# First product of the last layer pair as a block product for two of three token groups, and whole periods of the cosine written as integers by ScalarE

## Chip, cores and metric

One core of one Trainium2 chip runs the whole program in one launch. The metric is the device time of that launch in microseconds, lower is better; the number shown for a kernel is the median of several runs.

## What is computed

Three layers follow each other on 1152 tokens (2 x 576) of 512 channels: an attention with a bias from a small network, a mixture of four experts, and a last layer pair. The change touches the last pair alone:

```python
def _moe2_ref(x, w_in, w_out):      # x (1152, 512), w_in (512, 2048), w_out (2048, 512)
    h = x @ w_in
    g = h * np.cos(h)
    return (g @ w_out).astype(np.float32)
```

## The kernel before, in words

The program is written as a list of steps. A step names an engine, a duration that the author expects, what it reads and writes, and a function that issues its instructions. Graph.order() (line 107) is a planner: it plays the steps through with those expected durations, takes on each engine the ready step that stands first in the list, hands out buffers, and so fixes the order of instructions on every engine. Some steps may go to one of two engines; the planner decides. The engines run their queues in that order, and semaphores hold an instruction until its inputs are there. An instruction that waits holds all behind it on its engine.

Numbers of 32 bits are multiplied as pairs: a value is split into a high part (a copy rounded to the matmul's format) and a low part (the rest), and a product takes three matmuls: high x high, high x low, low x high. split (line 544) does that for weights: the high part on GpSimd or ScalarE (lines 546, 548), the low part on GpSimd or VectorE (line 549).

The experts' first product is done for most jobs as a block product (block_tokens line 804, block_weights line 856, block_job line 884): the tokens are cut into two column groups, the channels into two halves, the hidden units into two halves, and seven products of half size stand for eight, by Winograd's form of Strassen's rule. It needs sums of weights (S1 to S4), sums and differences of token groups (T1 to T4), and additions of products on VectorE (plus, line 906), some of which are kept in SBUF by ScalarE (keep_, line 902). Each block product is 6 matmuls (line 897).

The last pair goes in four pieces of 512 hidden units (jobs, line 1112, run by run_ff, line 764). In a piece, the three token groups of 384 (ALLG, line 985) take the first product plainly: l1_mm (line 750) is one step of 12 matmuls of 384 columns into one PSUM bank for 128 hidden units, four such steps a group. The second product l2_mm (line 756) is 12 matmuls of 512 columns for 128 tokens, three such steps a group, and follows one group behind. The first piece takes the token groups in reverse. Tokens come from the experts' layer in nine tiles of 128; each is transposed (line 972) and split into xh by ScalarE (line 975) and xl by VectorE (line 977).

Between the products stands m2_ev1 (line 1080), which makes h*cos(h). It finds the nearest whole number of periods by adding and subtracting a large constant (lines 1084 and 1086, ScalarE), takes 2 pi times that number away in two parts (lines 1088 and 1090, VectorE), takes the absolute value (1092) and the sine of pi/2 minus it (1093, both ScalarE), multiplies by h (1095, VectorE, reads PSUM) and splits the result (1096 ScalarE, 1097 VectorE). m2_ev2 (line 1102) adds up second products on VectorE (line 1108) and writes the output by DMA (line 1110).

Of the kernel before, what the change touches and what calls it, by code (L numbers as in the profile page):

```python
# [22 lines left out]
MAGIC = 12582912.0  # L23
# [312 lines left out]
def build(ctx: ExitStack, tc: tile.TileContext, consts, q, v, qd, kp, vp, w12, probs, mw1, mw2, win, wout, out):  # L336
# [28 lines left out]
    kc = T(sm, [128, 3], F32, "kc")  # L365
# [63 lines left out]
    G.step("DVE", 60, lambda: (nc.vector.memset(kc[:, 0:1], MAGIC), nc.vector.memset(kc[:, 1:2], float(np.pi / 2))), wr=[fix("kc")])  # L429
# [374 lines left out]
    def block_tokens(cols, keys, n, after):  # L804
# [4 lines left out]
        def block(d):  # L809
            ra, rb, rc, rd_ = [[(fix(nm), k) for nm in ("xh", "xl") for k in keys(dd, c)] for dd, c in ((d, 0), (d, 1), (d + 2, 0), (d + 2, 1))]  # L810
# [5 lines left out]
            def keep_(name, src, buf):  # L816
# [39 lines left out]
    def block_weights(srcs, after):  # L856

        fs = [Buf("F") for _ in range(4)]
        for f, src in zip(fs, srcs):
            dma(128 * 512 * 4, lambda f=f, src=src: nc.sync.dma_start(out=f.tile, in_=src), wr=[f], after=after)  # L860
        out = {}
        for d in range(2):
# [11 lines left out]
            for b, names in ((s12, ("S1", "S2")), (s34, ("S3", "S4")), (g, ("A12", "A22"))):  # L874
                h, l = Buf("W"), Buf("W")
                split(b, h, l, lambda h=h: h.tile, lambda l=l: l.tile, lambda b=b: b.tile, 512)
                for i, nm in enumerate(names):
                    out[nm, d] = (h, l), (lambda h=h, i=i: h.tile[:, 256 * i:256 * i + 256], lambda l=l, i=i: l.tile[:, 256 * i:256 * i + 256])
            h = Buf("W")
            split(f, h, h, lambda h=h: h.tile[:, lo_], lambda h=h: h.tile[:, hi_], lambda f=f: f.tile[:, lo_], 256)  # L880
            out["A11", d] = (h,), (lambda h=h: h.tile[:, lo_], lambda h=h: h.tile[:, hi_])
        return out

    def block_job(e, f0, cols, T_, n, gate):

        A = block_weights([mw1[e, 128 * i:128 * i + 128, f0:f0 + 512] for i in range(4)], [ends["bl"]] if "bl" in ends else gate)
        w2s = [load_w(mw2[e, f0 + 128 * i:f0 + 128 * i + 128, :], 512, (), [ends["l2"]]) for i in range(4)]
# [45 lines left out]
        ends["l1"] = ends["b1"]  # L933
        rd = [x for w in w2s for x in w[:2]]
# [97 lines left out]
    for i in blocked:  # L1032
        block_job(i // 2, 512 * (i % 2), bcols, tk, Q1, [last_l1[0]])
# [46 lines left out]
    def m2_ev1(n, z, hb):  # L1080
        h_, l_ = (lambda: hb.tile[:, 0:n]), (lambda: hb.tile[:, n:2 * n])
        m, r = Buf("F"), Buf("F")
        zz, mm_, rr = (lambda: z.tile[:, 0:n]), (lambda: m.tile[:, :n]), (lambda: r.tile[:, :n])
        G.step("ACT", t_act(n, 1), lambda: nc.scalar.activation(
            out=mm_(), in_=zz(), func=AF.Identity, scale=float(1 / (2 * np.pi)), bias=kc[:, 0:1]), rd=[z], wr=[m], new=[m, r])
# [4 lines left out]
        G.step("DVE", t_dve(n), lambda: nc.vector.scalar_tensor_tensor(  # L1090
            out=rr(), in0=mm_(), scalar=-C2, in1=rr(), op0=ALU.mult, op1=ALU.add), rd=[m, r], wr=[r], port=True)
# [10 lines left out]
    def m2_ev2(c, tt, y, c0, m):  # L1102
# [105 lines left out]
```

## Time and profile before

| | us |
|---|---|
| median of 3 runs | 810.33 (810.1 to 814.82) |
| span of the profiled execution, first to last instruction | 806.9 |
| TensorE busy | 787.3 |
| VectorE busy | 624.9 |
| ScalarE busy | 458.5 |
| GpSimd busy | 281.0 |
| last layer pair, from the first matmul of it to the last | 604.7 to 803.8 |

The profiled execution shows its span; what lies around it in a run is read as the difference to the median, 3.4 us. Busy times are from the profile: the time in which an engine had an instruction at work. Matmuls overlap in their pipeline, so a matmul's own duration says less than the distance between two.

### The profile page before, as it was taken

How to read it: one execution, taken by the hardware profiler on the slowest of the kernel's cores; microseconds unless marked ns; L12 is line 12 of the kernel's file. 1: busy time of each engine (PE TensorE's matmuls, PEld its weight loads, DVE VectorE, ACT ScalarE, POOL GpSimd, SP SyncE). 2: the span in 40 equal slices, each digit the busy share in tenths (PEclk: the TensorE clock that was granted, in tenths of full speed). 3: DMA queues.
4: the chain of work that ended last, by engine and by line, in shares of the span. 5: the costliest groups of instructions: out<-in, count | busy, mean ns of one | idle time of the engine just before them, and what ended most of it. 6: DMA issues, size and time to landing. Idle time of an engine off the chain costs nothing.

```text
span 806.9 us, 14934 instructions
## 1 busy us (share of the span) xinstructions
PE 787.3 (98%) x5190; PEld 654.6 (81%) x5190; DVE 624.9 (77%) x1376; ACT 458.5 (57%) x961; POOL 281.0 (35%) x292
## 2 busy tenths in 40 slices
PE   7899999999999999999999999999999999999998
PEld 5575667877888878888788888888889899998997
DVE  8969998888897887788887878777648655676664
ACT  6667547777786752335452626161428776675662
POOL 0110055658776873134451415050222130502200
PEclk9999999999999999999999999999999999999999
DMA  6978989877664520556434353444301110301112
GB/s 218 290 255 246 284 296 297 275 242 232 199 192 141 173 86 4 181 186 221 168 115 157 124 156 125 153 128 145 103 14 53 41 52 1 105 1 54 51 40 79
DMA packets 79275, 118.72 MB, mean 147 GB/s; under 512 B 12000, under 2 KB 37216, under 8 KB 79200
## 3 DMA queue, kind: packets, MB, share of 16 engines
q1 hardware_dynamic: 79200, 117.77, 45.5%
q8 instruction: 41, 0.67, 0.3%
q14 instruction: 34, 0.28, 0.1%
HBM read 96.00 MB, written 21.73 MB: 146 GB/s over the span
## 4 chain that ended last, share of the span: by engine, by line
PE 89%; DVE 7%; issue 2%; DMA 1%; ACT 1%; POOL 1%; SPq 0%; DVEq 0%; ACTq 0%; POOLq 0%
PE p1x L762 24%; PE p1x L753 11%; PE p L762 9%; PE p L753 9%; PE p1x L897 9%; PE p L700 4%; PE p L637 4%; PE p L506 4%; PE p L682 3%; PE p L897 3%; PE p L998 3%; PE p L1006 3%; PE p L658 1%; DVE es L514 1%; DVE es L521 1%
## 5 line engine op out<-in xcount | busy, mean ns | idle before, releaser
L762 PE MATMUL p1x<-wx,hs 128*128 128x512 f32 x882 | 205.9, 389 | 0.0
L762 PEld LDWEIGHTS p1x<-wx,hs 128*128 128x128 f32 x882 | 164.3, 188 | 33.4
L549 POOL TENSOR_TENSOR wx<-fs,wx 128x512 fp32r<-128x512 f32 (+1 forms) x82 | 100.3, 1234 | 28.3 <-ACT wx L548 26.0
L753 PE MATMUL p1x<-xh,wx 128*128 128x384 f32 (+2 forms) x344 | 97.3, 351 | 1.6 <-DVE hs L949 1.6
L546 POOL TENSOR_SCALAR wx<-fs 128x512 fp32r<-128x512 f32 (+1 forms) x29 | 16.5, 572 | 200.4 <-DMA fs<-in_mw 97.9
L762 PE MATMUL p<-wx,hs 128*128 128x512 f32 (+1 forms) x342 | 82.5, 388 | 0.9 <-DVE fs L963 0.9
L628 POOL TENSOR_SCALAR es<-es,stats 128x576 f32<-128x576 f32 x72 | 54.6, 762 | 79.2 <-ACT bs L485 30.1
L762 PEld LDWEIGHTS p<-wx,hs 128*128 128x128 f32 x342 | 62.8, 188 | 14.2 <-DVE fs L963 1.3
L753 PE MATMUL p<-xh,wx 128*128 128x384 f32 (+2 forms) x264 | 73.5, 344 | 0.3 <-DVE fs L705 0.3
L753 PEld LDWEIGHTS p1x<-xh,wx 128*128 128x128 f32 x344 | 63.0, 188 | 6.8 <-DVE hs L949 2.1
L621 ACT ACTIVATE es<-es,stats 128x576 f32<-128x576 f32 x72 | 55.4, 770 | 10.0 <-DVE stats L618 6.8
L506 PE MATMUL p<-bs,wpc 128*32 128x288 bf16 (+3 forms) x1152 | 53.8, 321 | 6.9 <-DVE es L521 3.6
L753 PE MATMUL p1x<-xl,wx 128*128 128x384 f32 (+2 forms) x172 | 60.2, 350 | 0.0
L548 ACT ACTIVATE wx<-fs 128x512 fp32r<-128x512 f32 (+1 forms) x84 | 49.0, 595 | 17.1 <-DMA fs<-wout 5.4
L618 DVE CUSTOM_DVE_ANT_0 es<-p,es 128x576 f32<-128x576 f32 x72 | 53.3, 750 | 3.9 <-PE p L649 1.7
L506 PEld LDWEIGHTS <-wpc 128*32 128x32 bf16 x1152 | 30.7, 96 | 28.8 <-issue 18.3
L753 PEld LDWEIGHTS p<-xh,wx 128*128 128x128 f32 x264 | 48.0, 188 | 2.7 <-DVE fs L705 0.6
L557 DVE TENSOR_TENSOR hs<-p,hs 128x512 fp32r<-128x512 f32 x62 | 42.5, 689 | 9.9 <-ACT hs L555 9.0
L948 ACT ACTIVATE hs<-p1x 128x512 fp32r<-128x512 f32 (+2 forms) x42 | 24.2, 579 | 41.3 <-PE p1x L753 30.7
L481 DVE TENSOR_SCALAR bs<-cst,cneg 128x576 bf16<-128x576 f32 (+3 forms) x108 | 46.7, 470 | 0.0
L637 PE MATMUL p<-ident,es 128*128 128x128 f32 x280 | 43.2, 279 | 2.0 <-DVE fs L705 0.7
L753 PE MATMUL p<-xl,wx 128*128 128x384 f32 (+2 forms) x132 | 45.1, 341 | 0.0
(233 smaller groups left out, 1662.8 us busy)
## 6 DMA issues: line engine op xcount, KB each, us to landing
fs<-in_mw SPq DMA_DIRECT2D x117, 256.0 KB, 3.9
es<-biasD SPq DMA_DIRECT2D x24, 288.0 KB, 4.0
fs<-in_wout SPq DMA_DIRECT2D x24, 256.0 KB, 3.0
fs<-in_win SPq DMA_DIRECT2D x22, 256.0 KB, 3.4
es<-in_kp SPq DMA_DIRECT2D x16, 288.0 KB, 4.2
es<-biasD SPq DMA_DIRECT2D x16, 256.0 KB, 3.6
es<-biasD SPq DMA_DIRECT2D x16, 224.0 KB, 3.9
biasD<-es SPq DMA_DIRECT2D x12, 288.0 KB, 4.4
```

The lines of the kernel that those rows point to most:

```text
L481: e.tensor_scalar(out=mask(t), in0=tab[:, w0:w0 + W], scalar1=cneg[:, u:u + 1], scalar2=None, op0=ALU.is_ge)
L506: nc.tensor.matmul(out=pv(a)[32 * t:32 * t + 32], lhsT=wpc[:, i, 32 * kk:32 * kk + 32], rhs=mask(t, m * a, m), start=(i == 0), stop=(i == ...
L548: alts=[("ACT", t_act(n, 0, 1), lambda: nc.scalar.activation(out=hv(), in_=fv(), func=AF.Copy), P_SPA)], off=O_SPL)
L549: low = lambda e: e.tensor_tensor(out=lv(), in0=fv(), in1=hv().bitcast(F32), op=ALU.subtract)
L557: G.step("DVE", t_dve(n), lambda: nc.vector.tensor_tensor(out=dst(AL), in0=src(), in1=dst(AH).bitcast(F32), op=ALU.subtract), rd=[ps_, (AH ...
L618: G.step("DVE", t_dve(S) + 10, lambda: nc.vector.tensor_tensor_reduce(out=f3(bt.tile[:, :S]), in0=sp.tile[:, :, 0:288], in1=f3(bt.tile[:, ...
L621: exp_all.append(G.step("ACT", t_act(S, 1, 1) + 67, lambda: nc.scalar.activation(out=e.tile[:, :S], in_=bt.tile[:, :S], func=AF.Exp, scale ...
L628: nrm = lambda g: g.tensor_scalar(out=e.tile[:, :S], in0=e.tile[:, :S], scalar1=stats[:, 3, c:c + 1], scalar2=1.0, op0=ALU.mult, op1=ALU.mult)
L637: nc.tensor.transpose(tp.tile[:, 128 * kt:128 * kt + 128], e.tile[:, 128 * kt:128 * kt + 128], ident)
L753: nc.tensor.matmul(out=z.tile[:, 0:n], lhsT=w[dt][2][wi]()[:, 128 * ft:128 * ft + 128], rhs=x[:, dt, p0:p0 + n], start=(dt == 0 and i == 0 ...
L762: nc.tensor.matmul(out=y.tile[:, 0:m], lhsT=hx, rhs=w[ft][2][wi]()[:, c0:c0 + m], start=(ft == 0 and i == 0), stop=(ft == nf - 1 and i == 2))
L897: nc.tensor.matmul(out=z.tile[:, 0:n], lhsT=x()[:, 128 * t:128 * t + 128], rhs=y(), start=(start and d == 0 and i == 0), stop=(d == 1 and ...
```

## The change

In the last pair, each of the four pieces now takes token group 0 (tokens 0 to 383 of the kernel's order) plainly, and groups 1 and 2 as the two column groups of a block product, 384 columns wide. block_weights splits the four plain weight tiles as well as the sums S1 to S4; block_tokens forms T1 to T4 once, from the experts' output. The second product of group 0 stands between the last but one and the last products, that of group 2 behind them, and that of group 1 behind the next piece's plain group 0. The last expert job takes its second products for the first token group in reverse, so that the tiles 3 and 4 are done before 2 and 1.

In m2_ev1 the first ScalarE instruction writes its result as 32-bit integers, of h/(2 pi) + 1/4, and VectorE's two instructions read these integers; the subtraction of the large constant and the absolute value are gone, and the sine takes the reduced value plus pi/2. At the program's start ScalarE converts 0.75 and -0.75 the same way, and VectorE makes the constant pi/2 from the two results.

```diff
+    whole = kc[:, 5:7].bitcast(I32)
+    G.step("DVE", 120, lambda: (nc.vector.memset(kc[:, 0:1], 0.25), nc.vector.memset(kc[:, 3:4], 0.75), nc.vector.memset(kc[:, 4:5], -0.75)), wr=[fix("kc")])
+    G.step("ACT", 100, lambda: nc.scalar.activation(out=whole, in_=kc[:, 3:5], func=AF.Copy), rd=[fix("kc")], wr=[fix("kc")], prio=10 ** 5)
...
-    def block_weights(srcs, after):
+    def block_weights(srcs, after, full=False):
...
+        if full:
+            for i, f in enumerate(fs):
+                h, l = whole(f)
+                plain[i] = h, l, (lambda h=h: h.tile, lambda l=l: l.tile)
+                halves(h, l, ("A12", "A22") if i > 1 else ("A11", "A21"), i % 2)
...
-            for j in range(n // 128):
+            for j in range(n // 128) if c or not last else reversed(range(n // 128)):
...
         G.step("ACT", t_act(n, 1), lambda: nc.scalar.activation(
-            out=mm_(), in_=zz(), func=AF.Identity, scale=float(1 / (2 * np.pi)), bias=kc[:, 0:1]), rd=[z], wr=[m], new=[m, r])
-        G.step("ACT", t_act(n, 0, 1), lambda: nc.scalar.activation(
-            out=mm_(), in_=mm_(), func=AF.Copy, bias=-MAGIC), rd=[m], wr=[m])
+            out=turns(), in_=zz(), func=AF.Identity, scale=float(1 / (2 * np.pi)), bias=kc[:, 0:1]), rd=[z], wr=[m], new=[m, r])
         G.step("DVE", t_dve(n), lambda: nc.vector.scalar_tensor_tensor(
-            out=rr(), in0=mm_(), scalar=-C1, in1=zz(), op0=ALU.mult, op1=ALU.add), rd=[m, z], wr=[r])
+            out=rr(), in0=turns(), scalar=-C1, in1=zz(), op0=ALU.mult, op1=ALU.add), rd=[m, z], wr=[r])
...
-        G.step("ACT", t_act(n, 0, 1), lambda: nc.scalar.activation(out=rr(), in_=rr(), func=AF.Abs), rd=[r], wr=[r])
         G.step("ACT", t_act(n, 1, 1), lambda: nc.scalar.activation(
-            out=rr(), in_=rr(), func=AF.Sin, scale=-1.0, bias=kc[:, 1:2]), rd=[r], wr=[r])
+            out=rr(), in_=rr(), func=AF.Sin, bias=kc[:, 1:2]), rd=[r], wr=[r])
...
+    for c in range(4):
+        A, plain = block_weights([(w_in_[128 * i:128 * i + 128, 512 * c:512 * c + 512], conv.get(("i", c, i), ())) for i in range(4)],
+                                 [ends["bl"]], True)
...
+        if c == 0:
+            tk2.append(block_tokens(pcols, lambda d, x: range(3 * x + 3, 3 * x + 6), NP, [], ("x2h", "x2l"), "t4b"))
...
+        for ft in range(4):
+            z = Buf("P1")
+            ends["l1"] = G.step("PE", 12 * t_mm(NP), lambda z=z, plain=plain, ft=ft: l1_mm(z, plain, ft, 0, NP),
+                                rd=[x for w in plain for x in w[:2]] + xr2(0, NP), wr=[z])
+            m2_ev1(NP, z, h0[ft])
+        for f in later:
+            f()
+        hbs = block_products(A, tk2[0], NP, m2_ev1, lambda: l2(0, h0))
+        l2(2 * NP, hbs[1])
+        later = [lambda l2=l2, hbs=hbs: l2(NP, hbs[0])]
```

block_products is the part of block_job that issues the seven products and their evacuations, taken out as a function of its own, with the evacuation as an argument.

The next pieces show how the order moves. TensorE at the start of the last pair, before: the four transposes of the last token tile (L972) stand between plain steps (L753).

```order
L753 MATMUL p1x_4013<-xl,wx_4221 128x384
L753 MATMUL p1x_4013<-xh,wx_4220 128x384
L972 MATMUL p1x_4035<-ident,fs_98 128x128 x4
L753 MATMUL p_153<-xh,wx_3035 128x384
L753 MATMUL p_153<-xl,wx_3035 128x384
```

The same place after, where L1000 are the transposes and L911 the block products:

```order
L911 MATMUL p1x_4016<-xl,wx_3250 128x384
L911 MATMUL p1x_4016<-xh,wx_3251 128x384
L1000 MATMUL p_153<-ident,fs_104 128x128 x4
L911 MATMUL p1x_4038<-xh,wx_2973 128x384
L911 MATMUL p1x_4038<-xl,wx_2973 128x384
```

One block product now stands ahead of the transposes and two behind them; the four plain steps (L757) of group 0 follow, and then the products that read T1 to T4.

VectorE behind the last token tiles (the L977 rows), before, where the evacuation of the last pair (L1088 to L1097) begins at once:

```order
L977 TENSOR_TENSOR xl<-p1x_4035,xh 128x4x128 x2
L1088 SCALAR_TENSOR_TENSOR fs_107<-fx_4186,p1x_4013 128x384
L1090 SCALAR_TENSOR_TENSOR fs_107<-fx_4186,fs_107 128x384
L1088 SCALAR_TENSOR_TENSOR fs_106<-fs_98,p_153 128x384
L1090 SCALAR_TENSOR_TENSOR fs_106<-fs_98,fs_106 128x384
```

VectorE after, from the last token tile (L1005) on; L804 are steps that form T1 to T4, L1115 the first instruction of an evacuation:

```order
L1005 TENSOR_TENSOR xl<-p_153,xh 128x4x128
L804 TENSOR_TENSOR fs_111<-fs_111,fx_4189 128x384
L804 TENSOR_TENSOR fs_99<-xh,fs_101 128x384
L804 TENSOR_TENSOR fx_4189<-xh,fs_111 128x384
L804 TENSOR_TENSOR tx_4327<-fs_101,tx_4328 128x384
L804 TENSOR_TENSOR fs_99<-fs_99,xl 128x384
L804 TENSOR_TENSOR tx_4405<-fs_111,tx_4406 128x384
L804 TENSOR_TENSOR fx_4189<-fx_4189,xl 128x384
L804 TENSOR_TENSOR xl<-fs_99,xh 128x384
L804 TENSOR_TENSOR fs_111<-xh,fx_4189 128x384
L1115 SCALAR_TENSOR_TENSOR fs_100<-fs_101,p_153 128x384
L921 TENSOR_TENSOR p1x_4037<-p1x_4037,fs_108 128x384
```

Nine token steps now stand between the last token tile and the first evacuation.

GpSimd at the same place, before, where it only splits weights (L546, L549):

```order
L546 TENSOR_SCALAR wx_4197<-fs_102 128x512
L549 TENSOR_TENSOR wx_4196<-fs_102,wx_4197 128x512
L549 TENSOR_TENSOR wx_4192<-fs_101,wx_4193 128x512
L546 TENSOR_SCALAR wx_3251<-fs_111 128x512
L549 TENSOR_TENSOR wx_3252<-fs_111,wx_3251 128x512
```

GpSimd after:

```order
L804 TENSOR_TENSOR fs_111<-fs_111,fx_4189 128x384
L804 TENSOR_TENSOR fs_99<-fs_99,fs_98 128x384
L804 TENSOR_TENSOR tx_4227<-fs_99,tx_4228 128x384
L804 TENSOR_TENSOR fs_99<-fs_99,fs_101 128x384
L804 TENSOR_TENSOR fs_101<-xh,fs_99 128x384
L804 TENSOR_TENSOR fs_101<-fs_101,xl 128x384
L553 TENSOR_TENSOR wx_4199<-fs_98,wx_4200 128x512
L804 TENSOR_TENSOR tx_4298<-fx_4189,tx_4299 128x384
L553 TENSOR_TENSOR wx_4195<-fs_102,wx_4196 128x512
```

Seven token steps now lie in GpSimd's queue, all but one of them ahead of the low halves (L553) of the first piece's second weights.

## Rows read from the trace of the kernel before

**Rows 1.** The page: span; busy time of each engine over the span
```profile
span 806.9 us, 14934 instructions
...
PE 787.3 (98%) x5190; PEld 654.6 (81%) x5190; DVE 624.9 (77%) x1376; ACT 458.5 (57%) x961; POOL 281.0 (35%) x292
```

**Rows 2.** Busy us in stretches: PE, PEld, DVE, ACT, POOL; then clock, DMA share, GB/s
```profile
0.00:100.00 100.00, 91.38 (x1181) 60.47 (x1182) 88.55 (x220) 66.10 (x136) 8.62 (x15) 1.00 0.82 259
100.00:200.00 100.00, 96.78 (x942) 77.33 (x940) 85.57 (x237) 67.34 (x157) 62.54 (x74) 1.00 0.84 269
...
400.00:500.00 100.00, 100.00 (x442) 82.78 (x442) 79.39 (x167) 46.65 (x91) 34.56 (x34) 1.00 0.45 144
...
604.00:804.00 200.00, 199.78 (x1030) 182.64 (x1028) 128.65 (x227) 132.97 (x271) 39.19 (x32) 1.00 0.14 47
604.00:649.30 45.30, 45.30 (x240) 41.82 (x239) 31.92 (x53) 35.37 (x73) 11.27 (x11) 1.00 0.18 59
649.30:699.00 49.70, 49.70 (x254) 45.37 (x253) 31.21 (x56) 34.04 (x69) 11.19 (x10) 1.00 0.11 37
```

**Rows 3.** The chain that ended last, 560 us to the end: start, us, what
```profile
570.00 4.08 PE p1x L897 x18
...
626.65 2.72 PE p L762 x12
...
701.02 4.16 PE p L753 x24
...
795.47 2.72 PE p1x L762 x12
```

**Rows 4.** Who waited for whom, TensorE, 395 to 807 us: total, times, longest
```profile
PE p1x L897 <- DVE fs L963: 0.4, 1, 0.4
```

**Rows 5.** Groups of VectorE, 350 to 600 us: count, busy us, mean ns
```profile
L1067 DVE SCALAR_TENSOR_TENSOR fs<-fs 128x256 f32<-128x256 f32 x42 | 18.7, 446 | 1.5
...
L549 DVE TENSOR_TENSOR wx<-fs,wx 128x512 fp32r<-128x512 f32 x19 | 15.2, 818 | 0.0
...
L1061 DVE SCALAR_TENSOR_TENSOR fs<-fs,fs 128x256 uint32<-128x256 uint32 x31 | 13.1, 424 | 0.3
...
L800 DVE TENSOR_TENSOR fs<-fs,fs 128x256 f32<-128x256 f32 x9 | 3.7, 417 | 0.0
```

**Rows 6.** Groups of VectorE, 604 us to the end
```profile
L1095 DVE TENSOR_TENSOR fs<-p1x,fs 128x384 f32<-128x384 f32 x9 | 4.9, 555 | 0.2 <-ACT fs L1093 0.2
```

**Rows 7.** Busy time of line 1090 alone (VectorE), 604 to 804 us
```profile
604.00:804.00 200.00, 29.00 (x48) 1.00 0.14 47
```

**Rows 8.** In order of time, GpSimd, then VectorE: start, us
```profile
608.92 1.30 POOL L549 TENSOR_TENSOR wx<-fs,wx 128x512 fp32r<-128x512 f32 x1 [2.65 <-ACT wx L548]
609.13 1.50 DVE L1090 SCALAR_TENSOR_TENSOR fs<-fx,fs 128x384 f32<-128x384 f32 x1
...
616.99 0.55 DVE L1088 SCALAR_TENSOR_TENSOR fs<-fx,p 128x384 f32<-128x384 f32 x1
617.47 0.55 DVE L1090 SCALAR_TENSOR_TENSOR fs<-fs,fs 128x384 f32<-128x384 f32 x1
```

**Rows 9.** Groups of ScalarE, 604 us to the end
```profile
L1086 ACT ACTIVATE fs<-fs 128x384 f32<-128x384 f32 x30 | 15.4, 515 | 0.2
...
L548 ACT ACTIVATE wx<-fs 128x512 fp32r<-128x512 f32 x13 | 8.0, 622 | 5.4 <-DMA fs<-wout 5.4
```

**Rows 10.** Groups of GpSimd, first row 604 us to the end, second 350 to 600
```profile
L549 POOL TENSOR_TENSOR wx<-fs,wx 128x512 fp32r<-128x512 f32 x16 | 22.2, 1394 | 8.4 <-ACT wx L548 7.4 <-DMA fs<-wout 0.4
L800 POOL TENSOR_TENSOR fs<-fs,fs 128x256 f32<-128x256 f32 x7 | 6.3, 894 | 7.6 <-DVE fs L800 2.7 <-ACT fs L1052 2.5 <-DVE hs L949 2.3
```

**Rows 11.** In order of time, the first 3 us
```profile
0.74 1.28 ACT L444 ACT_TABLE_LOAD   x1 [0.74 <-PEq L1201]
...
2.75 0.29 DVE L442 TENSOR_SCALAR cneg<-prm 128x144 f32<-128x144 f32 x1 [1.73 <-DMA prm<-in_w]
```

**Rows 12.** In order of time, VectorE near the end
```profile
793.40 0.55 DVE L1097 TENSOR_TENSOR hs<-fs,hs 128x384 fp32r<-128x384 f32 x1
```

More of the change, by code (lines that the diff above doesn't have):

```diff
@@ L22 @@
 NTOK, DM, NE, FF, FF2 = B * S, 512, 4, 1024, 2048
-MAGIC = 12582912.0
 C1 = 6.28125
@@ L802, in two, with block_tokens @@
                       alts=[("DVE", t_dve(n), lambda: f(nc.vector), P_TWO)], port=True, **kw)
-    def block_tokens(cols, keys, n, after):
+    def block_tokens(cols, keys, n, after, names=("xh", "xl"), t4n="t4"):
         c0, c1 = cols
@@ L809, in block @@
         def block(d):
[L810 removed]
+            ra, rb, rc, rd_ = [[(fix(nm), k) for nm in names for k in keys(dd, c)] for dd, c in ((d, 0), (d, 1), (d + 2, 0), (d + 2, 1))]
             u, v, w = Buf("F"), Buf("F"), Buf("F")
@@ L854, in block_tokens, with whole, halves @@
         return out
-    def block_weights(srcs, after):
+    def block_weights(srcs, after, full=False):
         fs = [Buf("F") for _ in range(4)]
-        for f, src in zip(fs, srcs):
-            dma(128 * 512 * 4, lambda f=f, src=src: nc.sync.dma_start(out=f.tile, in_=src), wr=[f], after=after)
-        out = {}
+        for f, (src, need) in zip(fs, srcs):
+            dma(128 * 512 * 4, lambda f=f, src=src: nc.sync.dma_start(out=f.tile, in_=src), wr=[f], after=list(need) + list(after))
+        out, plain = {}, [None] * 4
+        def whole(b):
+            h, l = Buf("W"), Buf("W")
+            split(b, h, l, lambda: h.tile, lambda: l.tile, lambda: b.tile, 512)
+            return h, l
+        def halves(h, l, names, d):
+            for i, nm in enumerate(names):
+                out[nm, d] = (h, l), (lambda i=i: h.tile[:, 256 * i:256 * i + 256], lambda i=i: l.tile[:, 256 * i:256 * i + 256])
+        if full:
[3 more added lines that the diff above has]
+                halves(h, l, ("A12", "A22") if i > 1 else ("A11", "A21"), i % 2)
         for d in range(2):
@@ L873, in block_weights, with block_products @@
             two(v(s34, hi_), v(g, lo_), v(s12, hi_), ALU.subtract, [g, (s12, 2)], [(s34, 4)], 256)
[L874 to L887, printed above, removed]
+            for b, names in ((s12, ("S1", "S2")), (s34, ("S3", "S4"))) + (() if full else ((g, ("A12", "A22")),)):
+                halves(*whole(b), names, d)
+            if not full:
+                h = Buf("W")
+                split(f, h, h, lambda h=h: h.tile[:, lo_], lambda h=h: h.tile[:, hi_], lambda f=f: f.tile[:, lo_], 256)
+                out["A11", d] = (h,), (lambda h=h: h.tile[:, lo_], lambda h=h: h.tile[:, hi_])
+        return out, plain
+    def block_products(A, T_, n, evac, mid=None):
         hbs = {c: [None] * 4 for c in range(2)}
@@ L926, in block_job @@
             hidden_(t, 1, 1, st[t]["p5"], True)
-            z = prod(t, "b", "A12", "B21", True)
-            plus(z, st[t]["p1"], z)
-            hidden_(t, 0, 0, z)
+            if mid is None:
+                z = prod(t, "b", "A12", "B21", True)
+                plus(z, st[t]["p1"], z)
+                hidden_(t, 0, 0, z)
+        if mid is not None:
+            mid()
+            for t in range(2):
+                z = prod(t, "b", "A12", "B21", True)
+                plus(z, st[t]["p1"], z)
+                hidden_(t, 0, 0, z)
         for t in range(2):
@@ L933, in block_job @@
         ends["l1"] = ends["b1"]
+        return hbs
+    def block_job(e, f0, cols, T_, n, gate, last):
+        A, _ = block_weights([(mw1[e, 128 * i:128 * i + 128, f0:f0 + 512], ()) for i in range(4)], [ends["bl"]] if "bl" in ends else gate)
+        w2s = [load_w(mw2[e, f0 + 128 * i:f0 + 128 * i + 128, :], 512, (), [ends["l2"]]) for i in range(4)]
+        hbs = block_products(A, T_, n, moe_ev1)
         rd = [x for w in w2s for x in w[:2]]
         for c in (1, 0):
-            for j in range(n // 128):
+            for j in range(n // 128) if c or not last else reversed(range(n // 128)):
                 y = Buf("P1")
```

40 lines of the change are left out of this document (27 added, 13 removed).

## The prediction

> **What bounds the kernel now.** I read the page first: TensorE is busy for 98% of a span of 806.9 us [rows 1]. Busy matmuls can still be waiting, so the next view is the busy time by stretch: from 400 us on TensorE is at 100%, while VectorE, the next busiest, is at 79% between 400 and 500 us and at 64% over the last layer pair (128.65 of 200 us) [rows 2]. Then the chain that ended last: in the last pair it is made of TensorE pieces alone, of two kinds. A step of the second product (12 matmuls, 512 columns) takes 2.72 us, that is 226.7 ns a matmul; two steps of the first product (24 matmuls, 384 columns) take 4.16 us, that is 173.3 ns [rows 3]. The view of waits closes it: from 395 us to the end TensorE waited once, 0.4 us [rows 4]. So the last pair lasts as long as its matmuls do, and a matmul removed there is time removed, if the other engines keep up with the faster pace.
>
> **TensorE, the gain.** One of the four pieces of the last pair has, before, 4 steps of 12 matmuls for each of three token groups: 144. After, group 0 still takes 4 steps (48), and groups 1 and 2 together take 7 block products for each of two halves, 6 matmuls each: 84 instead of 96. That is 12 fewer in a piece, 48 in all, and the instruction orders agree (5844 rows before, 5796 after). A block product has the same shape as what it replaces. That the block form runs at the pace of its width is seen in the blocked expert jobs: 18 of its matmuls of 512 columns take 4.08 us, 226.7 ns each, as in the second product [rows 3]. So the gain is 48 x 173.3 ns = 8.3 us. It can't be more by a shorter evacuation, because nothing waits for one now [rows 4].
>
> **ScalarE.** Two instructions of 0.515 us go from each of 48 evacuations (the subtraction of line 1086 and the absolute value of line 1092, of one form): 96 x 0.515 = 49 us [rows 9]. Added are 24 copies that keep a product (about 0.51 us, taken as the same), 8 copies of formed tokens, and 20 more high halves of weights at 0.622 us [rows 9]: 12 + 4 + 12 = 28 us. ScalarE falls from 133 to about 112 us [rows 2]; it is no bound. The evacuation chain becomes two links shorter.
>
> **VectorE.** The four instructions of an evacuation stay. Added are, by the order: 24 additions of products at 0.555 us [rows 6] = 13.3; of the 28 steps that form the tokens 21 land on VectorE, at 0.55 us [rows 8] = 11.6; 12 sums of weights of 256 columns at 0.417 us and 5 more low halves at 0.818 us [rows 5] = 5.0 + 4.1. Together 34 us on 128.65. It is not spread evenly. Pieces 2 to 4 get (13.3 + 5.0 + 4.1)/4 = 5.6 us each: 31.2 + 5.6 = 36.8 us in 49.7 - 2.1 = 47.6 us, 77% [rows 2]. The stretch of 400 to 500 us has 79%, with the same kind of block products, and lost nothing [rows 2]: I take nothing lost there. The first piece is another matter. It had 31.9 us of VectorE in 45.3 us [rows 2]; it gets 3.3 us of additions and the 13 of the 21 token steps that the order puts from the last token tile but one on (7.2 us): 42.4 us in 43.2, or 98%. Its weight sums mostly stand ahead of the pair, where VectorE has room. The products that need formed tokens start 8.3 us after the plain group 0, so those steps have a deadline, and in front of them, in VectorE's queue, nothing can be overtaken: the evacuations of group 0, and through them the second product, are queued behind. Bounds for what TensorE loses: nothing, as at 79%; or what it loses where VectorE is fuller, 3.2% at 86% (100 to 200 us) and 8.6% at 89% (0 to 100 us, where the first loads are waited for too) [rows 2]. On 43.2 us that is 0, 1.4 or 3.7 us. I take 2.0, near the stretch from 100 to 200 us, which has no such start.
>
> **GpSimd.** It gets 11 more low halves at 1.39 us, 20 sums of 256 columns at 0.89 us [rows 10] and 7 token steps (about 1.1 us, between those two), and loses 4 high halves (about 0.7): 15 + 18 + 8 - 3 = 38 us on 39 [rows 2]. It has the time; the question is whom it disturbs. The row that shows it: line 1090 on VectorE takes 0.55 us [rows 8], but the one that began at 609.13, within GpSimd's instruction of 608.92 to 610.22, took 1.50 [rows 8]. Its 48 instructions took 29.0 us where 48 x 0.55 = 26.4 would do [rows 7]: 2.6 us, 0.054 us each, at GpSimd's 39 us.
>
> The Trainium skill, "SBUF — State Buffer", section "SBUF: two separate sides", says that VectorE and GpSimd share a pair of ports under an exclusive lock: a VectorE instruction with two SBUF inputs and a GpSimd instruction don't share, whichever starts second waits for the whole of the first. This speaks against the change, which adds instructions with two SBUF inputs to both. The trace agrees (1.50 us for 0.55, until 0.41 us past the end of the other). What it would make of the time is the second rival below.
>
> **Edits at nothing.** The three constants and their conversion at the start put one instruction of ScalarE ahead of VectorE's queue. ScalarE's table load ends at 2.02 us, and VectorE's next work waits for a load until 2.75 us [rows 11]: 0.7 us of cover for one narrow instruction; without it, at most 0.3 us. Reading the whole periods as integers: integer operands cost VectorE no more than floats where the trace has both (424 ns against 446, 256 columns) [rows 5]; the mixed form itself isn't in the trace, and its bad end is the third rival. At the end, the last second-product steps need hidden tiles whose last one was ready at 793.95, 1.5 us ahead of 795.47 [rows 12, 3]. After the change four evacuations follow four products of 1.04 us and not four steps of 2.08, but three second-product steps (8.2 us) still cover them: 21 VectorE instructions at a spacing of 0.47 to 0.48 us [rows 8] are 10 us against 3.1 + 8.2 = 11.3 us. I take nothing; without that cover it is up to 2 us. The group order of the first piece also changes: the plain group 0 needs the token tile that is finished last. TensorE has three block products that need no formed tokens for that gap, 3 x 1.04 us, of which two stand behind the last transposes: 2.1 us, while the copy and subtraction of that tile take 1.3 us plus two hand-overs. It just fits.
>
> **The sum.** 806.9 - 8.3 + 2.0 = 800.6 us of span. The median of the runs, 810.33 us, is 3.4 us above this profiled span, so the forecast is 804.0 us, 0.8% below. A measurement of this kernel can tell about 1% (8.1 us) from no change, so this forecast counts as within 1%; faster by over 1% means below 802.2.
>
> **Rival 1, the whole gain.** The first piece loses nothing: VectorE's queue stays just ahead, as it does at every other place from 400 us on. For it: one wait of 0.4 us in 400 us [rows 4], and two fewer links in each chain. Against: 98% of VectorE in that piece. Time: 810.3 - 8.3 = 802.0, by a hair more than 1%.
>
> **Rival 2, the engines that share the work disturb each other and eat the gain.** If what an instruction pays grows with GpSimd's time (77 against 39 us), it is 0.107 us, and about 139 instructions of the pair have two SBUF inputs (48 + 48 + 21 + 12 + some 10), against 100 before: 14.9 - 5.4 = 9.5 us more, 2.4 in each piece. The first piece then has 44.8 us of VectorE in 43.2: 1.6 us over, and the 3.7 us that the fullest stretch lost. The others have 39.2 of 47.6 us, 82%, between the stretch that lost nothing and the one that lost 3.2%: 1.4 us each at the bad end. 1.6 + 3.7 + 4.2 = 9.5: 802.0 + 9.5 = 811.5. Against: the order keeps two such instructions apart where it can.
>
> **Rival 3, slower: mixed integer reads at half pace.** If VectorE needs a second pass over the integer operand (lines 1115 and 1117 of the new kernel), an instruction of 384 columns, spaced at 0.47 us now [rows 8], costs up to as much again; I take 0.4. 96 x 0.4 = 38 us, 9.6 a piece: 46.4 of 47.6 us in pieces 2 to 4 and 52.0 of 43.2 in the first. The first runs 8.8 us over; the others, at 97%, lose more than the 8.6% seen at 89%, say 6 us each: 802.0 + 8.8 + 18 = 829. It decides once VectorE passes what a piece of TensorE lasts. Against: the equal pace of integer and float instructions above.
>
> **Chances.** Forecast (802.2 to 806) 0.47; rival 1 0.27; rival 2 (806 to 818) 0.20; rival 3 or the like 0.06. Range: from rival 1 with a run's spread, 801.3, to most of rival 2, 810.0; above it lie about 0.15, below it 0.04. Faster by over 1% is rival 1, 0.27; slower by over 1% is rival 3, 0.06; within 1% the rest, 0.67.
>
> **What would show it.** Right: 48 fewer matmuls of 384 columns at 173 ns; ScalarE near 112 us and VectorE near 160 us in the last pair; TensorE's only waits in the first piece, for VectorE, 1 to 3 us in sum. Wrong: waits of TensorE in every piece (rival 2, with long forms of lines 1117 and 1123 beside GpSimd), a mean of line 1115 far above 0.55 us (rival 3), or a wait for the last token tile at the pair's start.

## The result, and the profile after

The changed kernel takes 821.97 us (median of 4 runs, 818.9 to 823.77) beside 810.28 us for the kernel before: a ratio of 1.0138, 95% interval 1.0112 to 1.0164. It is slower. The forecast was 804.0 us, with 801.3 to 810.0 as its range.

The page of the changed kernel, beside [rows 1]:

```profile
span 819.3 us, 14908 instructions
PE 786.7 (96%) x5142; PEld 648.2 (79%) x5142; DVE 668.0 (82%) x1440; ACT 443.5 (54%) x918; POOL 320.5 (39%) x326
```

The 48 matmuls are gone (5142 for 5190). So the work shrank as planned, and the time went up. Where? The busy time by stretch (PE, PEld, DVE, ACT, POOL, then the granted clock), the last pair as a whole and then its four pieces, beside the last rows of [rows 2]:

```profile
604.00:816.00 212.00, 199.19 (x984) 176.35 (x983) 163.75 (x275) 113.65 (x219) 72.00 (x60) 0.98 0.13 44
605.00:650.00 45.00, 40.39 (x204) 36.78 (x203) 42.81 (x71) 33.19 (x67) 22.93 (x19) 0.96 0.13 42
650.00:703.00 53.00, 49.09 (x244) 43.40 (x244) 38.14 (x63) 28.51 (x55) 20.75 (x18) 1.00 0.13 40
703.00:756.00 53.00, 48.97 (x241) 42.74 (x240) 41.63 (x68) 27.34 (x53) 21.79 (x18) 1.00 0.13 41
756.00:816.00 60.00, 59.74 (x294) 52.64 (x293) 40.22 (x74) 24.61 (x47) 6.05 (x5) 0.97 0.14 53
```

TensorE was full here before; now it idles 4.6, 3.9, 4.0 and 0.3 us in the four pieces, and its clock is below 1 in the first and the last. The last piece, where GpSimd has 6.05 us of work in place of 21 to 23, hardly idles. The pair runs from 605.36 to 816.14 us, 210.8 us; before it took 199.1, and without 8.3 us of matmuls it would take 190.8. Of the 20.0 us lost, 12.8 are idle time and 3.4 a lower clock (added up over stretches of 2 us: the length less TensorE's busy time, and the length times one less the granted clock). The rest, 3.8 us, was not taken apart. The longest of TensorE's waits from 395 us on (total, times, longest), beside the single one of [rows 4]:

```profile
PE p1x L766 <- DVE fs L1121: 7.0, 4, 2.0
PE p L911 <- DVE fs L1121: 2.3, 1, 2.3
PE p L766 <- DVE fs L1121: 1.8, 1, 1.8
```

These three rows, 11.1 us, are waits for VectorE's multiplication by the cosine (line 1121): it gives back the PSUM bank that the next product writes. What stands in front of it on VectorE at the wait of 2.3 us, in order of time, GpSimd first (start, us), beside [rows 8]:

```profile
614.82 4.40 POOL L553 TENSOR_TENSOR wx<-fs,wx 128x512 fp32r<-128x512 f32 x3
616.45 1.64 DVE L1117 SCALAR_TENSOR_TENSOR fs<-fs,fs 128x384 f32<-128x384 int32 x1
618.01 1.62 DVE L1117 SCALAR_TENSOR_TENSOR fx<-fs,fx 128x384 f32<-128x384 int32 x1
...
620.02 0.55 DVE L1121 TENSOR_TENSOR fs<-p,fs 128x384 f32<-128x384 f32 x1
```

Two subtractions that read SBUF twice take 1.64 and 1.62 us while GpSimd makes low halves; line 1121, which reads PSUM, takes its 0.55, ends at 620.57, and TensorE goes on at 620.62. The 48 instructions of line 1117 add up to 39.94 us, where line 1090 had 29.00 [rows 7]:

```profile
604.00:816.00 212.00, 39.94 (x48) 0.98 0.13 44
```

And the clock, in the chain that ended last (start, us), behind that wait:

```profile
620.62 2.29 PE p L911 x6
622.91 1.49 PE p1x L911 x6
624.40 1.05 PE p L911 x6
```

Three steps of six matmuls of one shape take 2.29, then 1.49, then 1.05 us. The granted clock in the two stretches of 2 us from 620 on:

```profile
620.00:622.00 2.00, 1.38 (x4) 1.38 (x5) 2.00 (x6) 1.98 (x5) 0.00 (x0) 0.58 0.00 0
622.00:624.00 2.00, 2.00 (x8) 2.00 (x8) 1.83 (x4) 0.49 (x1) 0.00 (x0) 0.57 0.04 8
```

Both are means over a change of level: from 621 to 623 us it stands at 0.50, the level of 1.2 GHz. So this wait of 2.3 us costs TensorE more than 2.3 us. Not every such wait does. Behind the wait of 2.0 us that ends at 649.0 the clock stays at 1.00 (TensorE's busy time, then the clock):

```profile
646.00:648.00 2.00, 1.02 (x5) 1.00 0.00 0
648.00:650.00 2.00, 1.00 (x4) 1.00 0.00 0
```

The fall in the last piece comes behind a wait of 1.8 us that followed one of 1.6. What decides whether the clock falls, beside the length of the wait, stays open.

### The profile page after: what moved, and what is told of

The parts are those of the page before. It is cut to its first block, busy times and chain, and to the rows that moved or that the text cites. A ratio compares the mean times of both kernels' runs of the same rounds, so it can differ in the third digit from the quotient of the medians.

```text
span 819.3 us, 14908 instructions
## 1 busy us (share of the span) xinstructions
PE 786.7 (96%) x5142; PEld 648.2 (79%) x5142; DVE 668.0 (82%) x1440; ACT 443.5 (54%) x918; POOL 320.5 (39%) x326
## 4 chain that ended last, share of the span: by engine, by line
PE 69%; DVE 21%; issue 3%; ACT 3%; DMA 3%; POOL 1%; SPq 0%; DVEq 0%; ACTq 0%; POOLq 0%
PE p1x L766 18%; PE p1x L911 11%; PE p L766 7%; PE p1x L757 5%; PE p L911 5%; PE p L510 4%; PE p L704 3%; PE p L641 3%; PE p L686 3%; PE p L1026 3%; PE p L1034 3%; DVE fs L1117 2%; PE p L757 2%; DVE hs L1123 2%; DVE fs L1121 2%
## 5 line engine op out<-in xcount | busy, mean ns | idle before, releaser
L766 PE MATMUL p1x<-wx,hs 128*128 128x512 f32 (+1 forms) x834 | 195.3, 390 | 7.2 <-DVE fs L1121 7.0
L553 POOL TENSOR_TENSOR wx<-fs,wx 128x512 fp32r<-128x512 f32 (+1 forms) x94 | 119.4, 1283 | 50.1 <-ACT wx L552 44.5
L766 PE MATMUL p<-wx,hs 128*128 128x512 f32 (+1 forms) x390 | 95.7, 395 | 2.7 <-DVE fs L1121 1.8
L550 POOL TENSOR_SCALAR wx<-fs 128x256 fp32r<-128x256 f32 (+1 forms) x26 | 13.7, 534 | 164.7 <-DMA fs<-in_mw 35.5
L757 PE MATMUL p1x<-xh,wx 128*128 128x512 f32 (+2 forms) x240 | 69.1, 359 | 2.5 <-DVE hs L977 2.2
L911 PE MATMUL p1x<-xh,wx 128*128 128x512 f32 (+1 forms) x192 | 62.1, 371 | 0.7 <-DVE fs L1134 0.7
L757 PEld LDWEIGHTS p1x<-xh,wx 128*128 128x128 f32 x240 | 44.2, 189 | 8.5 <-DVE hs L977 2.9
L911 PE MATMUL p1x<-tx,wx 128*128 128x512 f32 (+1 forms) x216 | 50.5, 372 | 0.3 <-DVE fs L991 0.3
L911 PEld LDWEIGHTS p1x<-tx,wx 128*128 128x128 f32 x216 | 40.0, 191 | 6.1 <-issue 0.7
L757 PE MATMUL p1x<-xl,wx 128*128 128x512 f32 (+2 forms) x120 | 42.9, 357 | 0.0
```

Of the source, the lines that this page charges most:

```text
L553: low = lambda e: e.tensor_tensor(out=lv(), in0=fv(), in1=hv().bitcast(F32), op=ALU.subtract)
L757: nc.tensor.matmul(out=z.tile[:, 0:n], lhsT=w[dt][2][wi]()[:, 128 * ft:128 * ft + 128], rhs=x[:, dt, p0:p0 + n], start=(dt == 0 and i == 0 ...
L766: nc.tensor.matmul(out=y.tile[:, 0:m], lhsT=hx, rhs=w[ft][2][wi]()[:, c0:c0 + m], start=(ft == 0 and i == 0), stop=(ft == nf - 1 and i == 2))
L911: nc.tensor.matmul(out=z.tile[:, 0:n], lhsT=x()[:, 128 * t:128 * t + 128], rhs=y(), start=(start and d == 0 and i == 0), stop=(d == 1 and ...
```

## The experiments

The theories, as the expectations name them. T1: GpSimd's instructions hold up VectorE's instructions with two SBUF inputs. T2: VectorE simply has too much work. T3: the chain of the block form is too long in itself. Ratios are to the kernel before, run beside. "Lost" means idle time and clock of TensorE in the last pair, added up as above.

**The two halves of the change apart.** int_only is the kernel before with the integer cosine alone; block_only is the changed kernel with the old cosine.

> The kernel before with the integer form of the cosine alone; no block product. Three theories on why the change is slower: T1, VectorE's instructions with two SBUF inputs are held up by GpSimd's (line 1117 took 39.9 us for 48 in the changed kernel, against 29.0 for the same 48 instructions before); T2, VectorE simply has too much work in the last pair; T3, the chain from a block product through its addition and evacuation to the next product on the same bank is too long in itself. All three expect no change here: 810 us, plus or minus 4, TensorE without waits in the last pair, and the second subtraction near 29 us for 48. If the integer operand made that instruction longer, it would be near 40 us here too.

> The changed kernel with the cosine as before (adding and subtracting the large constant, absolute value); the block product stays. T1 and T2: like the changed kernel, 818 to 826 us, since VectorE and GpSimd have the same work. T3: slower than the changed kernel by some 5 us or more, because each evacuation has two links more on ScalarE (828 or more).

int_only took 812.88 us, 1.0042 (1.0028 to 1.0056), lost 0.8 us; block_only 813.29 us, 1.0047 (1.0032 to 1.0063), lost 7.4 us, all of it idle. Neither half makes the 1.4% alone. In int_only the second subtraction's 48 add up to 31.83 us, near 29 and not near 40, so the integer operand is not what makes them long. block_only came out as none of the three theories had expected (818 us or more). Its second subtraction's 48 add up to 28.0 us, not 39.94: with two more passes on ScalarE the order is another, and fewer of them meet GpSimd. Other instructions were held there, a multiplication (line 1119), for example, for 1.64 us in all. Of its 7.4 us, 2.9 stay with GpSimd barred from pieces 2 to 4 (hybrid_old_cos, below). What the integer cosine costs by itself is 0.4%; its trace shows four waits of 1.1 us in sum, and why there are any stayed open.

**GpSimd out of the pair; one subtraction less.** no_pool bars GpSimd from the last pair; one_sub leaves line 1117 out and takes 2 pi away in one part (a less exact reduction); no_pool_one does both.

```diff
-        G.step("POOL", ..., lambda: low(nc.gpsimd), alts=[("DVE", ...)])
+        if not pool_ok[0]:
+            G.step("DVE", t_dve(n), lambda: nc.vector.tensor_tensor(out=lv(), ...))
...
-            out=rr(), in0=turns(), scalar=-C1, ...)
-            out=rr(), in0=turns(), scalar=-C2, in1=rr(), ...)
+            out=rr(), in0=turns(), scalar=-2.0 * np.pi, ...)
```

> The changed kernel with GpSimd barred from the last pair: high halves of its weights go to ScalarE, low halves, weight sums and token steps to VectorE. VectorE gets some 66 instructions more (about 33 us of issue time). T1: no VectorE instruction of 384 columns above 0.6 us, TensorE's waits fall from 13 us to under 5, 804 to 811 us. T2: slower than the changed kernel, 825 us or more, TensorE waiting more. T3: like the changed kernel, 818 to 826 us.

> The changed kernel with one subtraction of 2 pi times the whole periods instead of two (line 1117 left out, 48 VectorE instructions fewer; the reduced value has a slightly larger rounding error). T1 and T2 both expect most waits gone: VectorE loses 40 us of 164, 802 to 808 us. T3: a chain shorter by one link of about 0.6 us: 815 to 820 us.

> no_pool (GpSimd barred from the whole last pair) with one subtraction of the turns. Without GpSimd no collision is left, so what one_sub could not show is seen alone: is VectorE's amount of work the limit of piece 1? T2: piece 1 holds 12 evaluations, 12 x 0.54 = 6.5 us less on VectorE there; no_pool's loss of 12.1 us (7.0 idle and the 5.1 of clock that follow) shrinks by 5 to 10, span 799 to 804, time 802 to 807, ratio 0.991 to 0.997. T3 (a chain too long in itself, whatever VectorE's load): as no_pool, ratio 1.001 to 1.004.

no_pool took 811.45 us, 1.0025 (1.0015 to 1.0035), with 7.0 us of waits: just outside what T1 had expected (804 to 811, under 5 us), and far from the 818 and more of T2 and T3. Piece 1, and then pieces 2 to 4, by stretch:

```profile
604.00:650.00 46.00, 38.97 (x196) 35.62 (x195) 45.30 (x94) 32.98 (x66) 0.00 (x0) 0.89 0.13 41
650.00:806.00 156.00, 156.00 (x788) 140.69 (x786) 118.95 (x235) 83.26 (x160) 0.00 (x0) 1.00 0.14 48
```

From 650 us on TensorE never stops, though VectorE now does all the sums and low halves. So in pieces 2 to 4 the loss was GpSimd's instructions in VectorE's way, T1, and not VectorE's load. (The planner made a new order for this version; the dose, below, keeps the order.) All of no_pool's loss, 7.0 us idle and 5.1 of clock, lies in piece 1, where VectorE is busy for 45.3 of 46 us, as T2 has it for that piece.

one_sub was a surprise: 26 us less on VectorE, and 823.04 us, 1.0168 (1.0139 to 1.0196). It has waits of 4.7 us. Before one of them, in order of time, GpSimd first:

```profile
687.83 5.65 POOL L553 TENSOR_TENSOR wx<-fs,wx 128x512 fp32r<-128x512 f32 x4
...
687.85 1.69 DVE L1121 TENSOR_TENSOR hs<-fs,hs 128x384 fp32r<-128x384 f32 x1
689.47 1.48 DVE L804 TENSOR_TENSOR fx<-fs,fs 128x256 f32<-128x256 f32 x1
690.87 1.48 DVE L804 TENSOR_TENSOR fs<-fs 128x256 f32<-128x256 f32 x1
692.28 1.48 DVE L804 TENSOR_TENSOR fs<-fs,fs 128x256 f32<-128x256 f32 x1
693.68 0.68 DVE L1132 TENSOR_TENSOR fs<-p1x,fs 128x512 f32<-128x512 f32 x1
```

The two engines take turns, one instruction each. A sum of weights of 256 columns takes 1.48 us in place of the 0.41 that the same kernel shows for such a sum at 685.84, and line 1132, which TensorE waits for, stands behind four such turns. What counts here is how many held instructions stand ahead of a bank's last reader, not how much work VectorE has. (With an instruction less in each evaluation the planner made another order, in which such a row of turns stands ahead of line 1132 twice.) The clock behind that wait (stretches of 2 us, busy times as above, clock third from the end):

```profile
692.00:694.00 2.00, 0.00 (x0) 0.00 (x0) 2.00 (x3) 0.21 (x1) 2.00 (x3) 0.50 0.00 0
694.00:696.00 2.00, 1.59 (x5) 1.59 (x6) 0.83 (x2) 1.00 (x2) 2.00 (x2) 0.50 0.00 0
696.00:698.00 2.00, 2.00 (x8) 2.00 (x7) 1.02 (x2) 0.58 (x1) 0.12 (x1) 0.50 0.00 0
698.00:700.00 2.00, 2.00 (x10) 1.96 (x10) 1.22 (x3) 1.28 (x3) 0.00 (x0) 0.82 0.00 0
```

It stands at 0.50, the level of 1.2 GHz, and is still there some 4 us after the matmuls have begun again. In the whole pair one_sub loses 13.1 us idle and 10.2 of clock.

no_pool_one missed: 809.69 us, 0.9992 (0.9977 to 1.0008), lost 10.2 us against no_pool's 12.1, all in piece 1. T2 had expected 5 to 10 us less; 1.9 came. So the evaluations' share of VectorE's work is only a small part of what makes piece 1 late in these two kernels. What is left are mainly the token forms, all on VectorE here, which stand ahead of the evaluations; that they are the rest is argued and not shown. late_block, below, moves them.

**The dose.** pool_only gives the sums and low halves of pieces 2 to 4 to GpSimd alone. pool_quarters cuts each low half that GpSimd makes in the pair into four instructions, pool_halves into two; all_quarters cuts its sums and token forms as well.

```diff
-               lambda: low(nc.gpsimd)
+            for q in range(4):
+                c = slice(128 * q, 128 * q + 128)
+                nc.gpsimd.tensor_tensor(out=lv()[:, c], in0=fv()[:, c], in1=hv()[:, c].bitcast(F32), op=ALU.subtract)
```

> The changed kernel, with the sums and the low halves of pieces 2 to 4 of the last pair on GpSimd alone (the planner cannot give one of them to VectorE): GpSimd's part grows by some 14 instructions of 0.9 to 1.4 us, VectorE's shrinks by as many of 0.45 to 0.6 us. T1: more collisions; the second subtraction and the last one (39.94 and 32.82 us for 48 in the changed kernel) grow, time 823 to 835, ratio 1.015 to 1.03. T2: VectorE is relieved by some 7 us, time below the changed kernel's 822, ratio 1.005 to 1.012. T3: no change, 1.012 to 1.016.

> The changed kernel, with each 512-column low half that GpSimd makes in the last pair (1.3 to 1.4 us) issued as four of 128 columns; order and engines otherwise as in the changed kernel. T1, held for the length of the one GpSimd instruction that runs: a held VectorE instruction takes 0.55 + at most some 0.45 in place of 1.6, the second subtraction's sum falls from 39.94 to 28 to 34 us, time 808 to 817, ratio 0.998 to 1.009. T1, shared out in some other way (GpSimd takes its columns' time whatever their grouping): the sum stays near 40 us and the time at 820 to 826. T2 and T3: no change, 819 to 824.

> As pool_quarters, with two instructions of 256 columns in place of four of 128. There the longest held instruction of VectorE fell from 1.68 us (changed kernel) to 1.09 = 0.55 + the 0.53 of one GpSimd quarter, and the second subtraction's 48 from 39.94 to 32.67 us. Hold as long as the one GpSimd instruction that runs: a half of some 0.75 us gives a longest form near 1.3 us, a sum of 34 to 38 us, and a time between the two, 808 to 818 (ratio 0.999 to 1.010). If cutting alone did it, whatever the length: as pool_quarters, longest form near 1.1 us, time 804 to 808.

> pool_quarters, with the sums and token forms that GpSimd makes in the last pair cut into 128 columns as well (256 columns took 0.98 to 1.09 us, 384 took 1.21). If the 3.9 us that pool_quarters still lost are holds behind those: loss 0 to 2 us, time 803 to 806, ratio 0.991 to 0.996. If they are VectorE's amount of work, or GpSimd's own lateness with longer work: loss as before or more, ratio 0.996 to 1.000.

pool_only took 829.8 us, 1.0239 (1.0208 to 1.027), the second subtraction 43.48 us: more work taken off VectorE, and a slower kernel. That is T1 against T2. pool_quarters took 806.75 us, 0.9974 (0.9949 to 0.9998), below its expected 808 to 817, with the same work on the same engines as the changed kernel, and in the last pair with the same order on TensorE, VectorE and ScalarE, as have pool_halves and all_quarters. pool_halves took 813.15 us, 1.0059 (1.004 to 1.0079). The hold, from the by-form view of the second subtraction (ns: shortest, median, longest) in the changed kernel, pool_halves and all_quarters:

```profile
L1117 DVE SCALAR_TENSOR_TENSOR fs<-fs,fs x29: 543/554/1683, 616.4 to 804.2; 128x384 f32<-128x384 int32 x29
```

```profile
L1126 DVE SCALAR_TENSOR_TENSOR fs<-fs,fs x29: 537/558/1130, 615.1 to 795.9; 128x384 f32<-128x384 int32 x29
```

```profile
L1133 DVE SCALAR_TENSOR_TENSOR fs<-fs,fs x29: 543/794/853, 617.9 to 795.5; 128x384 f32<-128x384 int32 x29
```

and GpSimd's low halves in the same three:

```profile
L553 POOL TENSOR_TENSOR wx<-fs,wx x29: 1281/1297/1616, 609.1 to 778.4; 128x512 fp32r<-128x512 f32 x29
```

```profile
L562 POOL TENSOR_TENSOR wx<-fs,wx x58: 718/747/1061, 607.6 to 770.7; 128x256 fp32r<-128x256 f32 x58
```

```profile
L562 POOL TENSOR_TENSOR wx<-fs,wx x116: 444/460/822, 610.2 to 770.9; 128x128 fp32r<-128x128 f32 x116
```

The longest form is above an undisturbed 0.55 us by 1.13, 0.58 and 0.30 us; GpSimd's usual instruction takes 1.30, 0.75 and 0.46 us. The one is the other less 0.16 to 0.17 us each time: a VectorE instruction waits for the one GpSimd instruction that is running. (pool_quarters, which leaves the sums whole, has a longest form of 1.09 us beside a sum of 1.05, and 0.86 is its longest beside a quarter.) The Trainium skill, "SBUF — State Buffer", section "SBUF: two separate sides", has this as a lock taken for a whole instruction; the three lengths agree. The 48 second subtractions add up to 39.94, 35.20 and 32.53 us (32.67 in pool_quarters). pool_quarters' waits are at most 1.1 us long, and its clock is 1.00 throughout the pair: with short holds the clock's share of the loss goes too. Its runs scatter, from 804.22 to 812.69 us, since holds depend on what meets what; the profiled one (span 803.2, lost 3.9) is near the lower end.

all_quarters missed: 812.68 us, 1.0048 (1.0028 to 1.0068), lost 8.5 us, though its longest form is the shortest of all. Its waits are for the same multiplication, up to 2.4 us. Why cutting the sums and token forms makes it worse was not found; that cutting the low halves helps the time, and by length, stands on the other two.

**Versions that beat both.** hybrid lets GpSimd work for piece 1 and the token forms and bars it from pieces 2 to 4. hybrid_one takes one subtraction out as well, hybrid_old_cos has the old cosine, hybrid_quarters cuts what GpSimd makes in piece 1. late_block takes piece 1 plainly, makes the token forms beside it, and starts the block form with piece 2. before_barred is the control: the kernel before, with GpSimd barred from pieces 2 to 4.

```diff
             tk2.append(block_tokens(pcols, ..., NP, [], ("x2h", "x2l"), "t4b"))
+            pool_ok[0] = False
```

> The changed kernel, with GpSimd allowed for the weights of the first piece and the token forms of the last pair and barred from everything that is issued after them (pieces 2 to 4). no_pool lost 12.1 us of TensorE's time in the last pair (7.0 idle, 5.1 of clock), all of it in piece 1, where VectorE had no pause; its span without that loss is 809.2 - 12.1 = 797.1. T1 for pieces 2 to 4 and T2 for piece 1 (collisions there, too much VectorE work here): pieces 2 to 4 lose under 1 us, piece 1 loses 3 to 8 us as in the changed kernel (4.6 idle there, 605 to 650), span 800 to 805, time 803 to 808, ratio 0.993 to 0.999. T1 alone (GpSimd harms piece 1 as well): span near 809 or more, ratio 1.002 and up. T3 (the chain of the block form): losses in all four pieces again, ratio over 1.004.

> hybrid, and one subtraction of the turns in place of two (line 1117 of the changed kernel left out, 2 pi in one constant: the product is exact to fewer digits). Takes 48 instructions of 0.54 us off VectorE in a pair of some 190 us. T2 for piece 1: the loss there halves or goes, span 797 to 801, time 800 to 804, ratio 0.989 to 0.994. T1 alone: as hybrid within 1 us, since the collisions of piece 1 stay. If the surprise of one_sub (nothing gained by 26 us less on VectorE) comes from something other than GpSimd's instructions, such as the later form of the loop, this gains nothing over hybrid either.

> hybrid with the cosine of the kernel before (7 steps, three more passes per evaluation on ScalarE than... two in fact: 48 x 2 x 0.515 = 49 us more on ScalarE, none on VectorE). Says what the second half of the change is worth where nothing collides. T1 and T2 (VectorE decides, ScalarE had room): as hybrid within 2 us, 804 to 808, ratio 0.993 to 0.998. T3 (length of the chain): slower than hybrid by 3 us or more, ratio 0.998 to 1.005, with waits in all pieces as in block_only.

> hybrid, with what GpSimd still makes in piece 1 cut into 128 columns. hybrid lost 2.3 us of waiting and 1.7 of clock there and nothing later. If those are holds: loss under 1.5 us, time 802 to 804, ratio 0.990 to 0.993, the fastest with two constants. If VectorE's amount of work: as hybrid, ratio 0.993 to 0.997.

> A version made from what the runs showed: in the first of the last pair's four pieces all three token groups are multiplied plainly (as in the kernel before), the token forms are made beside it, and the block product starts with piece 2; GpSimd is barred once the weights of piece 1 are split. 36 matmuls of 173.3 ns are spared in place of 48: 6.2 us. T2 for piece 1 (token forms, weights' forms and 12 evaluations were too much for VectorE in one piece): nothing is lost in any piece, span 806.9 - 6.2 = 800.7, time 803 to 805, ratio 0.990 to 0.995, two constants kept. If the block form cannot run beside VectorE whatever its start, pieces 2 to 4 wait as well: ratio over 0.997.

> The kernel before, with GpSimd barred from pieces 2 to 4 of the last pair (its 26 or so low halves there go to VectorE, 0.7 us each). TensorE lost 0.4 us in this pair before, so there is nothing to gain: ratio 0.998 to 1.002 by T1, T2 and T3. If it is below 0.997, part of what hybrid gained is not the block product's.

| kernel | us, median | ratio (95%) | lost in the last pair, us |
|---|---|---|---|
| hybrid | 805.98 | 0.9945 (0.9923 to 0.9967) | 2.3 + 1.7 of clock |
| hybrid_one | 803.21 | 0.9913 (0.9886 to 0.9940) | 0.3 |
| hybrid_old_cos | 805.50 | 0.9950 (0.9937 to 0.9964) | 2.9 |
| hybrid_quarters | 804.82 | 0.9941 (0.9925 to 0.9957) | 1.8 |
| late_block | 805.51 | 0.9952 (0.9935 to 0.9969) | 0.6 |
| before_barred | 809.79 | 1.0004 (0.9990 to 1.0018) | 0.0 |

hybrid's pieces, the first in two parts, by stretch:

```profile
604.00:620.00 16.00, 15.09 (x88) 14.39 (x86) 15.69 (x25) 9.57 (x19) 10.37 (x8) 1.00 0.15 49
620.00:650.00 30.00, 28.64 (x133) 25.75 (x134) 28.12 (x62) 23.74 (x48) 0.00 (x0) 0.94 0.11 36
650.00:700.00 50.00, 50.00 (x253) 45.24 (x252) 39.29 (x80) 30.37 (x59) 0.00 (x0) 1.00 0.20 63
700.00:750.00 50.00, 50.00 (x252) 45.24 (x251) 44.13 (x88) 29.61 (x58) 0.00 (x0) 1.00 0.13 43
750.00:800.00 50.00, 50.00 (x260) 45.57 (x259) 37.38 (x72) 22.29 (x43) 0.00 (x0) 1.00 0.10 39
```

Keeping GpSimd out of three pieces turns 1.4% slower into 0.6% faster. VectorE is at 88% from 700 to 750 us and TensorE loses nothing: load alone does not make it wait. before_barred gains nothing, so the gain is the block product's. hybrid_old_cos is as fast as hybrid, so the chain's length (T3) costs nothing here, and the integer cosine brings nothing measurable in this version. What is left in hybrid's piece 1 is one wait of 2.3 us, again with two held subtractions in front of it (1.64 and 1.62 us, from 617.18 on). hybrid_quarters shortens the holds: the clock loss is gone, a wait of 1.7 us stays, and its 0.9941 lies where the expectation had put VectorE's amount of work. hybrid_one, which has no such subtraction, loses 0.3 us; that takes the holds and the work away together and does not tell them apart. late_block loses 0.6 us, all in piece 1, 0.4 of it for the last token tile, so there is room for the token forms once no product waits for them; its expected 803 to 805 was missed by a hair, with a profiled span of 805.0 for 800.7. Part of that difference is not the change's: from 4 to 604 us, which the versions hardly touch, TensorE idles 14.4 to 18.2 us in the profiled executions of this study, 15.4 in the kernel before and 17.8 in late_block, which has 2.1 us in one wait where the kernel before has 0.3:

```profile
PE p L648 <- POOL es L639: 2.1, 1, 2.1
```

hybrid_one has the lowest median, with the less exact reduction, and an interval that overlaps hybrid's; of those with both constants, hybrid, hybrid_quarters, hybrid_old_cos and late_block can't be told apart.

## Why the prediction was wrong

- **TensorE's gain**: right. 48 matmuls fewer; hybrid_one's pair, which loses 0.3 us, takes 192.1 us from its first product to its last matmul, 7.2 less than the kernel before, measured the same way (199.3).
- **The busy times**: ScalarE 113.65 us (said about 112) and GpSimd 72.00 (said 77) are right. VectorE's 163.75 (said 128.65 + 34 = 162.7) is right by luck: lines 1117 and 1123 take 39.94 + 32.82 us where lines 1090 and 1097 took 29.00 + 29.08, so 14.7 of the 35.1 us more are time in which these instructions were held, and the work added within the pair came to some 20 us and not 34. The prediction did not fail by putting too little work on VectorE.
- **Pieces 2 to 4, "I take nothing lost there"**: this step failed. I compared busy shares, 77% here with 79% in the stretch that lost nothing. hybrid with 88% loses nothing, the changed kernel with 72% (38.14 of 53 us; 78% of the 49.1 in which TensorE worked) loses 3.9 us in piece 2. The share says nothing of the order in which held instructions and a bank's last reader stand.
- **GpSimd, "the question is whom it disturbs"**: the mechanism was seen [rows 8] and rightly named, and rival 2 with its waits beyond the first piece is what came (in the last piece, with little on GpSimd, 0.3 us); its size was wrong. I scaled the mean excess of line 1090, 0.054 us, by GpSimd's time to 0.107. Line 1117 paid (39.94 - 48 x 0.545) / 48 = 0.29 us, line 1123 0.14. A mean over a pair in which the two engines seldom meet can't be scaled by busy time: where GpSimd has several instructions in a row, each VectorE instruction with two SBUF inputs pays for a whole one, 1.1 us, and the row at 609.13 [rows 8] had nearly that price, 0.95. Rival 2 gave 811.5 us; 822 came.
- **What no rival held**: TensorE's clock. Behind some of the longer waits the granted clock fell, which cost 3.4 us in the changed kernel and 10.2 in one_sub. The kernel before has hardly a wait after 395 us [rows 4] and its clock stays at 1.00 [rows 2], so its trace could not show it there.
- **The first piece, 2.0 us, bounds 0 to 3.7**: too small as the changed kernel ran (4.6 us idle and a clock of 0.96); with GpSimd out of the way later, hybrid lost 4.0 and hybrid_quarters 1.8. The reason given, token forms with a deadline ahead of group 0's evacuations, fits no_pool, no_pool_one and late_block, but none of them moves the token forms alone; in the changed kernel the first wait of the piece stands behind two held subtractions.
- **Rival 3**, integers read at half pace: refuted. Line 1115's undisturbed form, 24 of its instructions in two groups, has medians of 0.544 and 0.546 us.
- **Edits at nothing** (constants at the start, the last token tile, the end): as said. TensorE idles 15.5 us from 4 to 604 us, 15.4 before, and has no wait for the last token tile.

## What to carry to other kernels

When work is moved to GpSimd beside a VectorE that reads SBUF twice, don't price it by busy time: count the held instructions that stand in VectorE's queue ahead of the one that TensorE waits for, at one whole GpSimd instruction each. Shorter GpSimd instructions shorten the longest hold by as much, though all_quarters shows that cutting everything need not be faster; taking GpSimd out of the stretch can be faster although VectorE gets more to do. A wait of TensorE of 2 us or more can bring a lower clock behind it, and its price then is more than its length.

## What the runs showed of the hardware that was not expected

VectorE and GpSimd took strict turns where both had instructions ready: with 512 columns on GpSimd, a turn from start to start took 1.40 us beside a VectorE instruction of 0.41 us (one_sub) and 1.56 us beside one of 0.55 (the changed kernel). TensorE's granted clock stayed at 0.50 for some 4 us behind a wait of 4.7 us, and did not fall at all where no wait was over 1.1 us (pool_quarters); in pool_only it fell behind one wait of 3.5 us (at 700.66) and stayed at 1.00 behind another (at 756.46), so the length alone does not decide. A VectorE instruction that reads integers from SBUF and floats from PSUM takes 0.54 us for 384 columns, no more than one that reads floats alone [rows 8].
